# A Fourier mixing layer followed by a gated feed-forward: the first batch's rows on neighbouring partitions, and another order of the first steps

## The chip, the cores and the metric

The kernel runs on one core of a Trainium2 chip. A core has five engines that run their own instruction streams: TensorE (matmuls; PE in the profile, its weight loads PEld), VectorE (DVE), ScalarE (ACT), GpSimd (POOL) and SyncE (SP), which only issues transfers here. ScalarE issues some transfers too. Sixteen DMA engines move the data. On-chip memory has 128 partitions; the matmul results go to eight banks of 128 x 512 f32.

The metric is the device time of one launch in microseconds, the median of several runs. Each is one launch that does all of the work, weight preparation included.

## The reference

```python
def _attn_ref(x):                       # x: (8, 3008, 256), float32
    X = np.fft.fft(x, axis=1)
    X = np.fft.fft(X, axis=2)
    return X.real.astype(np.float32)

def _moe_ref(x, w_in, w_out):           # (24064, 256), (256, 2048), (2048, 256)
    h = x @ w_in
    g = h * (1.0 / (1.0 + np.exp(-1.702 * h)))
    return (g @ w_out).astype(np.float32)
```

The second takes the first's result as its 24064 rows. The kernel gets w_in and w_out in eight bytes for each number and makes floats of them itself.

## The kernel before

**Tiling.** The length 3008 is split as NA * NB = 47 * 64. A first stage transforms over the 47 (matmuls whose weights hold the cosines and sines), its result is spilled to a buffer Td in DRAM and read back in another layout (fill, into t4), and a second stage (stage2) transforms over the 64 and is turned by VectorE's transposes into pq. The transform over the 256 columns is never done on the data: it is multiplied into w_in once (fold_w, four pieces of 512 columns, result in wcs). After that the kernel is a feed-forward: hidden (matmuls of pq with wcs), rows (VectorE builds the second half of the hidden rows by symmetry, with the row nb that nyquist makes, and writes them to a ring "h" of four buffers), activate (the gated activation on ScalarE), product (matmuls with wo).

**Loops.** There are 8 batches * 3 blocks * 2 halves * 8 pairs = 384 steps. The first NP = 8 steps use plain products; from step 8 on the products with w_out are done by a scheme with seven products instead of eight, applied twice (the lines L621 to L701 of the profile).

**Who orders the work.** All instructions are in the order in which the program text issues them on each engine; there is no scheduler. A list SCRIPT says what is issued between the steps 0 to 7. Semaphores follow from what writes and reads what. Transfers take turns on eight semaphores, so that a transfer also waits until the one eight issues before it has landed.

**Start of the program (L864 to L945).** The rows of batch 0 go straight from x to a tile xt: load_first puts 48 rows (one for each of the 47, and one more) on partitions 0, 2, ... 94, load_mirror puts the mirrored rows on 33, 35, ... 127. Seven memsets clear xt ahead of it, since the matmuls read all 128 partitions. tab1, the table with the weights of this first stage, is loaded on 128 partitions in two parts. SP issues load_first, ScalarE load_mirror. Then w_in(0) (in two halves), tab2 and w_in(1) follow on SP. fold_first (VectorE) folds the columns in groups of four, mix_first (TensorE) makes two slots at a time and ScalarE copies them to buffers made[k], of which three are the first three buffers of the ring "h". After every second one, spill_first sends 16 of the 48 rows of both halves to Td, one half on SP's queue and one on ScalarE's. When all is there, fill(0, 0, 4) reads the first third of t4 back. The other 32 rows are spilled later on SP, behind w_out(0) and w_in(2).

**Weights.** A piece of w_in or w_out is made a float in five operations: sizes (absolute value of the high words, on ScalarE or VectorE), clamp (GpSimd), low (the low words, ScalarE), high (two operations on VectorE), finish (GpSimd, into wst for w_in and wo for w_out). halved(n) makes sum and difference of the two halves of a piece on VectorE, so that fold_w(n) needs four matmuls of 512 columns rather than eight. fold_w(0) is without it. first_row(n) makes small factors af1 and af2 out of wcs.

**Around the change.** Before step 0 come, in this order: in1's preparation, fold_w(0), halved(1), rotate (psr, the first matmul that needs t4), out0's preparation, stage2(0, 0), first_row(0), high(out0), load_in(3), finish_out(0), fold_w(1). In the steps: in2 in steps 0 and 1, product(0) and (1), out1 and in3 in step 3.

**Banks.** A matmul result takes a bank by the name of a tag: o0, o1 are kept for the products of a block's end, the six others are taken in turn from a list `spare`; a call may also name its bank.

```python
    def bank(name, tag=None):
        if tag is None:
            tag = spare.pop(0)
            spare.append(tag)
```

A warm matmul (L348) is one whose result is not used.

Of the kernel before, what the change touches and what calls it, by code (L numbers as in the profile page):

```python
# [34 lines left out]
NA, NB = 47, 64  # L35
# [26 lines left out]
def tables(S, D):  # L62
# [14 lines left out]
    low, high, back = w0[0:2 * NA:2], np.zeros((NA, NJ + 1, NG * NU, 2)), NJ - np.arange(1, NJ)  # L77
# [3 lines left out]
    w0[33:33 + 2 * NA:2] = high  # L81
    sign = np.ones((128, 4))
    sign[33:33 + 2 * NA:2] = -1.0
# [36 lines left out]
def kernel(ctx: ExitStack, tc, x, w_in, w_out, tab1, tab2, out):  # L120
# [162 lines left out]
    def at_rows(first, at, *dims):  # L283
        one = xt[first:first + 1]
        return bass.AP(one.tensor, one.offset + at * D, [[2 * xt[:].ap[0][0], NM]] + [list(d) for d in dims])
# [6 lines left out]
    def load_mirror(k):  # L292

        parts = ((1, 4), (28, 32)) if k == 0 else ((4 * k, 4 * k + 4), (28 - 4 * k, 32 - 4 * k))
        for lo, hi in parts:
            nc.scalar.dma_start(out=at_rows(33, lo, [D, hi - lo], [1, D]),
                                in_=view(x, (NB - lo) * D, [NB * D, NM], [-D, hi - lo], [1, D]))
        if k == 0:
            nc.sync.dma_start(out=at_rows(33, 0, [1, D]), in_=view(x, NJ * D, [NB * D, NM], [1, D]))
# [6 lines left out]
    def fold_first(g):  # L306

        t, e = xt[:, 4 * g:4 * g + 4, :], room[g]
        fwd, rev = t[:, :, 1:H], free(t, D - 1, [D, 4], [-1, H - 1])
        nc.vector.tensor_tensor(e[:, :, 0:H - 1], fwd, rev, op=ALU.subtract)  # L310
        if g not in BY_PE:
            nc.vector.tensor_tensor(fwd, fwd, rev, op=ALU.add)

    def mix_first(i):

        ps, ns = bank("ps1"), (2 * i + 2, 2 * i + 1) if i < 7 else (0, 15)
        for at, n in enumerate(ns):
            todo = [], []
            for c, slot in enumerate((n, NJ - n if n else 16)):
                o = ps[64 * c:64 * c + 64, at * D:(at + 1) * D]  # L320
                even, odd_ = (w[:, k * NM:k * NM + 64] for w, k in ((w0, slot), (odd, slot or NJ)))
                todo[c].append((o[:, H + 1:], odd_, room[slot // 4][:, slot % 4, 0:H - 1], True, True))
                folded = slot // 4 not in BY_PE
                todo[c].append((o[:, 0:H + 1], even, xt[:, slot, 0:H + 1], True, folded))
                if not folded:
                    todo[c].append((o[:, 1:H], even, free(xt[:, slot], D - 1, [-1, H - 1]), False, True))
# [40 lines left out]
    def stage2(b, blk):  # L367
# [14 lines left out]
        for u in range(NU):  # L382
            for cs in range(parts):
# [111 lines left out]
    def fold_w(n):  # L495
# [10 lines left out]
        for cs in range(2):  # L506

            nc.scalar.copy(wcs[cs][:, n * 512:(n + 1) * 512].rearrange("p (f c) -> p f c", f=4),
                           free(ps[cs][:], 0, [1, 4], [4, 128]))
# [344 lines left out]
    odd, w0 = flat[:, 0:n0], flat[:, 6176:6176 + n0 + 4]  # L854
# [10 lines left out]
    for lo, hi in (28, 32), (24, 28), (20, 24), (8, 12), (12, 20):  # L865
        nc.gpsimd.memset(xt[:, lo:hi, :], 0.0)
    nc.vector.memset(xt[:, 0:4, :], 0.0)
    nc.vector.memset(wcs[0][:, 0:512], 1.0)
    nc.vector.memset(xt[:, 4:8, :], 0.0)
    nc.vector.memset(ones[:], 0.0)  # L870
    nc.vector.memset(ones[0:1, :], 1.0)
    nc.scalar.activation(af2[0:1, 0:1], twos[0:1, 0:1], ACTF.Gelu_apprx_sigmoid)
# [3 lines left out]
                      in_=view(tab1, 0, [tab1.shape[1], 128], [28 * NM, 2], [1, ends]))  # L876
    for i in range(4):
        load_first(i)
        load_mirror(i)
        if i == 0:  # L880
            nc.sync.dma_start(out=w0[:, ends:28 * NM], in_=tab1[:, ends:28 * NM])
        if i == 1:
            odd_weights(NM, ends)
            odd_weights(28 * NM, n0)
# [9 lines left out]
    for i, need in enumerate(((0, 7), (1,), (6,), (2,), (5,), (3,), (4,), ())):  # L894
# [6 lines left out]
        if i % 2:  # L901
            spill_first(i // 2, 0, 16, (nc.sync, nc.scalar))
# [18 lines left out]
    sizes(in1, nc.vector)  # L921
    low(in1)
    for h0 in (0, 512):
        clamp(in1, h0, 512)
    for h0 in (0, 512):
        high(in1, h0, 512)
    for h0 in (0, 512):
# [3 lines left out]
    warm(1)  # L931
    fold_w(0)
    halved(1)
    rotate(0, 0, 4, nc.scalar.copy)
    prepare(out0)
    sizes(out0, nc.scalar)
    clamp(out0)
    low(out0)
    stage2(0, 0)
    first_row(0)  # L940
    spare.append(spare.pop(0))
    high(out0)
    load_in(3, nc.sync)
    finish_out(0)
    fold_w(1)  # L945
# [11 lines left out]
    for t, c in ((1, 2), (3, 3)):  # L957
        at(t, load_out, c, nc.sync)
# [13 lines left out]
    for b in range(B):  # L972
# [26 lines left out]
        for blk in range(NBLK):  # L999
# [7 lines left out]
        [(prepare, in2), (low, in2), (nyquist, 0, 0), (rows, 0, ((sizes, in2, nc.vector), (clamp, in2)))],  # L1007
        [(first_row, 1), (activate, 0), (rows, 1), (high, in2), (finish, in2)],
        [(activate, 1), (rows, 2), (halved, 2)],
        [(product, 0, 0, None), (product, 1, 0, None), (bounds, out1), (activate, 2), (bounds, in3), (rows, 3), (activate, 3),  # L1010
         (fold_w, 2), (high, out1), (finish, out1), (high, in3), (finish, in3)],
# [4 lines left out]
    for t in range(n + LAG):  # L1016
        if t < NP:
            if t == NP - 3:
                spare[:] = [tag for tag in spare if tag[0] == "o"] + ["b2"]
# [96 lines left out]
```

## Time and profile before

| | us |
|---|---|
| median of 3 runs | 1845.98 (1845.35 to 1847.09) |
| the profiled execution, whole | 1845.24 |
| its span, first to last instruction | 1843.5 |
| TensorE's mean granted clock | 0.997 of full |

The start of the profiled execution, by its trace:

| what | us from the span's start |
|---|---|
| clearing of xt on GpSimd | 0.73 to 6.1 |
| first loads of x issued (SP, ScalarE) | 2.05, 1.99 |
| last load of load_first landed | 16.4 |
| last mirrored rows landed | 19.39 |
| w_in(0), its halves landed | 20.42, 21.86 |
| last spill of 16 rows issued, landed (ScalarE) | 24.21, 26.58 |
| the same on SP | 24.20, 27.4 |
| fill of t4 issued, landed | 27.50, 31.59 |
| w_out(0), w_in(2) landed | 34.08, 38.70 |
| hidden(0), first matmul | 38.15 |
| product(0), first matmul | 47.26 |
| fold_w(1), fold_w(2), fold_w(3) on TensorE | 34.84, 54.16, 65.49 |

How to read the profile: the page has one execution, engine by engine, and the line of the program for each group of instructions (L191 is the helper `halves`, which records many matmuls; the tile's name tells which). The chain of waits follows the end of the execution back, at each step to what released it. A group's "waited for" tells which engine, line and tile ended an idle stretch. In the windows, each engine's busy time is followed by the number of its instructions; PEclk is the share of full speed that TensorE's clock had, and the DMA share is the mean busy share of the sixteen DMA engines.

### The profile page before, as it was taken

The numbers are of one execution on the slowest core, as the hardware profiler recorded it, in microseconds if no ns is written. First come the engines' busy times: TensorE is split into PE (matmuls) and PEld (weight loads), VectorE is DVE, ScalarE is ACT, GpSimd is POOL, SyncE is SP. The second block draws the span as 40 slices with busy tenths as digits, with TensorE's granted clock in tenths as the row PEclk, the third lists the DMA queues.
The fourth block names the chain that finished last, engine by engine and source line by source line (L and its number), as shares of the span: only waits on it lengthen the run. The fifth ranks groups of instructions, "written<-read, shape, count | busy, mean of one in ns | idle before, by whom it ended". The sixth has DMA issues, their size and how long they took to land.

```text
span 1843.5 us, 55849 instructions
## 1 busy us (share of the span) xinstructions
PE 1826.2 (99%) x23650; PEld 1398.9 (76%) x23650; DVE 1479.1 (80%) x1930; ACT 1139.4 (62%) x2231; POOL 997.7 (54%) x1068
## 2 busy tenths in 40 slices
PE   8999999999999999999999999999999999999998
PEld 4677777777777777777777777777777877778776
DVE  6888788887888778877888778878888788878874
ACT  4666656666666666666666666666656666556663
POOL 3785555554656546564456644666446654444442
PEclk9999999999999999999999999999999999999999
DMA  8721331114211151211502115020241102100101
GB/s 276 189 70 26 90 65 28 55 32 106 43 48 40 35 112 30 61 35 45 111 13 73 33 50 97 23 72 26 75 74 28 29 26 59 28 19 13 23 19 24
DMA packets 150841, 105.95 MB, mean 57 GB/s; under 512 B 106197, under 2 KB 131799, under 8 KB 150032
## 3 DMA queue, kind: packets, MB, share of 16 engines
q1 hardware_dynamic: 147760, 100.33, 22.6%
q8 instruction: 186, 3.05, 0.7%
q10 hardware_dynamic: 2832, 2.05, 0.5%
q14 instruction: 63, 0.52, 0.1%
HBM read 65.07 MB, written 48.05 MB: 61 GB/s over the span
## 4 chain that ended last, share of the span: by engine, by line
PE 95%; POOL 2%; DMA 1%; DVE 1%; issue 0%; ACT 0%; ACTq 0%; DVEq 0%; POOLq 0%; SPq 0%
PE x L191 35%; PE o L191 26%; PE low L701 25%; PE o L701 4%; PE ps L268 2%; PE ps L378 1%; DMA xt<-in_x_dram 1%; PE po L191 0%; DMA big<-in_moe_w_in_dram 0%; PE psw L501 0%; POOL wo L475 0%; PE pa L191 0%; POOL wo L493 0%; POOL big L632 0%; DMA t<-Td 0%
## 5 line engine op out<-in xcount | busy, mean ns | idle before, releaser
L632 POOL TENSOR_TENSOR big<-big 128x256 f32<-128x256 f32 (+1 forms) x376 | 353.6, 940 | 785.7 <-ACT big L624 672.2
L191 PE MATMUL x<-pq,wcs 128*64 128x256 f32 (+1 forms) x6016 | 768.8, 376 | 1.5 <-ACT g L614 0.9
L191 PE MATMUL o<-big,wo 128*64 128x256 f32 (+1 forms) x4800 | 621.0, 375 | 0.5 <-DVE big L639 0.5
L191 PEld LDWEIGHTS x<-pq,wcs 128*64 128x64 f32 x6016 | 414.1, 137 | 181.4 <-issue 15.6
L614 ACT ACTIVATE g<-x 128x512 f32<-128x512 f32 (+1 forms) x376 | 221.7, 590 | 380.1 <-PE x L191 378.9
L191 PEld LDWEIGHTS o<-big,wo 128*64 128x64 f32 x4800 | 341.8, 137 | 146.8 <-DVE big L639 0.9
L633 POOL TENSOR_TENSOR big<-big 128x256 f32<-128x256 f32 (+1 forms) x376 | 411.2, 1094 | 0.0
L621 DVE TENSOR_TENSOR big<-g,x 128x512 f32<-128x512 f32 (+1 forms) x376 | 250.7, 667 | 183.6 <-ACT big L617 183.4
L602 ACT ACTIVATE x<-nb,af 128x256 f32<-128x256 f32 (+1 forms) x752 | 353.0, 469 | 70.1 <-DVE pq L385 57.0
L701 PE MATMUL low<-big 128*64 128x128 f32 (+1 forms) x5888 | 381.4, 270 | 0.0
L701 PEld LDWEIGHTS low<-big 128*64 128x64 f32 x5888 | 336.9, 137 | 28.2
L617 ACT ACTIVATE big<-x 128x512 f32<-128x512 f32 (+1 forms) x376 | 219.2, 583 | 122.2 <-PE x L191 112.2
L663 DVE TENSOR_TENSOR big<-big 128x1024 f32<-128x1024 f32 (+1 forms) x184 | 235.4, 1280 | 65.9 <-PE low L701 43.1
L624 ACT ACTIVATE big<-big 128x512 f32<-128x512 f32 (+1 forms) x376 | 231.6, 616 | 34.9 <-DVE big L621 32.6
L701 PE MATMUL low<-big,wo 128*64 128x128 f32 (+1 forms) x2944 | 220.3, 270 | 0.1
L665 DVE TENSOR_TENSOR big<-big 128x512 f32<-128x512 f32 (+1 forms) x184 | 179.6, 976 | 16.3 <-DVE big L663 0.5
L667 DVE TENSOR_TENSOR big<-big 128x512 f32<-128x512 f32 (+1 forms) x184 | 184.0, 1000 | 0.0
L701 PEld LDWEIGHTS low<-big,wo 128*64 128x64 f32 x2944 | 171.8, 137 | 4.2 <-DVE big L667 0.5
L640 DVE TENSOR_TENSOR big<-big 128x512 f32<-128x512 f32 (+1 forms) x188 | 143.3, 762 | 6.5
L639 DVE TENSOR_TENSOR big<-big 128x512 f32<-128x512 f32 (+1 forms) x188 | 131.2, 698 | 3.5 <-POOL big L632 3.5
L803 DVE TENSOR_TENSOR big<-big,low 128x512 f32<-128x512 f32 (+3 forms) x184 | 109.0, 609 | 3.8
L701 PEld LDWEIGHTS o<-big,wo 128*64 128x64 f32 x1472 | 92.3, 137 | 24.9
(104 smaller groups left out, 1100.5 us busy)
## 6 DMA issues: line engine op xcount, KB each, us to landing
out_dram<-os SPq DMA_DIRECT2D x284, 64.0 KB
t<-Td SPq DMA_DIRECT2D x22, 512.0 KB
Td<-xt SPq DMA_DIRECT2D x56, 192.0 KB
xt<-in_x_dram SPq DMA_DIRECT2D x14, 512.0 KB
xt<-Xr SPq DMA_DIRECT2D x14, 512.0 KB
nb<-Nd SPq DMA_DIRECT2D x23, 256.0 KB
out_dram<-os SPq DMA_DIRECT2D x96, 56.0 KB
Xr<-in_x_dram SPq DMA_DIRECT2D x7, 752.0 KB
```

The costliest lines, as they stand in the source:

```text
L191: nc.tensor.matmul(out[c0:c0 + 64], lhsT=lhs[:, c0:c0 + 64], rhs=rhs, skip_group_check=True, **how)
L602: nc.scalar.activation(x[:, i * 256:i * 256 + n], nbt[b, blk][:, hh * 256:hh * 256 + n], ACTF.Copy, scale=af1[:, f:f + 1])
L614: nc.scalar.activation(two(g[:], n), two(xb[t][:], n), ACTF.Copy, scale=2.0)
L617: nc.scalar.activation(front(t), two(xb[t][:], width(t)), ACTF.Gelu_apprx_sigmoid)
L621: nc.vector.tensor_tensor(back(t), two(gt.pop(t)[:], n), two(xb.pop(t)[:], n), op=ALU.subtract)
L624: nc.scalar.activation(back(t), back(t), ACTF.Gelu_apprx_sigmoid)
L632: eng.tensor_tensor(right(t, S1, n), left(t, A21, n), right(t, A22, n), op=ALU.add)
L633: eng.tensor_tensor(left(t, S3, n), left(t, A11, n), left(t, A21, n), op=ALU.subtract)
L663: nc.vector.tensor_tensor(free(big[:], SUM, *both_), free(big[:], from11 + w, *twice), free(big[:], from11, [at_right(t, 0) + w - from11, ...
L665: nc.vector.tensor_tensor(s2, a11, s1, op=ALU.subtract)
L667: nc.vector.tensor_tensor(s4, a12, s2, op=ALU.subtract)
L701: nc.tensor.matmul(o, lhsT=lhs, rhs=rhs, start=first_in, stop=(p == NP - 2), skip_group_check=True)
```

## The change

1. The rows of batch 0 lie on partitions 0 to 47 and their mirrored rows on 48 to 95, and all operations of the first stage read 96 partitions. The seven memsets of xt are gone; tab1's first part is loaded on 96 partitions.
2. The load of ScalarE's activation table (with a first Gelu of one element) stands behind its first four transfers instead of ahead of them.
3. Both halves of the first spills are issued on ScalarE's queue.
4. The sizes of in1 are made on ScalarE in two halves of 512, not on VectorE in one; its low comes later. fold_w(0) is issued without its copies; the two copies (keep) stand before and behind rotate.
5. Ahead of step 0 only stage2(0, 0) and first_row(0) are left. out0's preparation, halved(1) and load_in(3) are in step 0, fold_w(1) and in2's sizes in step 1, in2's high and finish in step 3, with load_out(2) and load_out(3), which were tied to steps 1 and 3.
6. After fold_w(0) the list of spare banks is written out by name, 22 entries long; at step 5 it is set to four names.
7. In stage2's first block the four transposes go by column half first.

```diff
-    w0[33:33 + 2 * NA:2] = high
+    w0[NM:NM + NA] = high
...
     def at_rows(first, at, *dims):
         one = xt[first:first + 1]
-        return bass.AP(one.tensor, one.offset + at * D, [[2 * xt[:].ap[0][0], NM]] + [list(d) for d in dims])
+        return bass.AP(one.tensor, one.offset + at * D, [[xt[:].ap[0][0], NM]] + [list(d) for d in dims])
...
-        for u in range(NU):
-            for cs in range(parts):
+        for cs in range(parts):
+            for u in range(NU):
...
-    def fold_w(n):
+    def fold_w(n, copy=True):
...
-        for cs in range(2):
-
-            nc.scalar.copy(wcs[cs][:, n * 512:(n + 1) * 512].rearrange("p (f c) -> p f c", f=4),
-                           free(ps[cs][:], 0, [1, 4], [4, 128]))
+        folded_w[n] = ps
+        if copy:
+            keep(n, 0)
+            keep(n, 1)
+
+    folded_w = {}
+
+    def keep(n, cs):
+        nc.scalar.copy(wcs[cs][:, n * 512:(n + 1) * 512].rearrange("p (f c) -> p f c", f=4),
+                       free(folded_w[n][cs][:], 0, [1, 4], [4, 128]))
...
-    for lo, hi in (28, 32), (24, 28), (20, 24), (8, 12), (12, 20):
-        nc.gpsimd.memset(xt[:, lo:hi, :], 0.0)
-    nc.vector.memset(xt[:, 0:4, :], 0.0)
     nc.vector.memset(wcs[0][:, 0:512], 1.0)
-    nc.vector.memset(xt[:, 4:8, :], 0.0)
...
-    nc.scalar.activation(af2[0:1, 0:1], twos[0:1, 0:1], ACTF.Gelu_apprx_sigmoid)
...
-                      in_=view(tab1, 0, [tab1.shape[1], 128], [28 * NM, 2], [1, ends]))
+                      in_=view(tab1, 0, [tab1.shape[1], 2 * NM], [28 * NM, 2], [1, ends]))
...
         if i == 1:
+            nc.scalar.activation(af2[0:1, 0:1], wcs[0][0:1, 0:1], ACTF.Gelu_apprx_sigmoid)
...
-            spill_first(i // 2, 0, 16, (nc.sync, nc.scalar))
+            spill_first(i // 2, 0, 16, (nc.scalar, nc.scalar))
...
     prepare(in1)
-    sizes(in1, nc.vector)
-    low(in1)
     for h0 in (0, 512):
+        sizes(in1, nc.scalar, h0, 512)
         clamp(in1, h0, 512)
     for h0 in (0, 512):
         high(in1, h0, 512)
+    warm(1)
+    fold_w(0, False)
+    spare[:] = ["b0", "b1", "b2", "o2", "b0", "o3", "o4", "o2", "b1", "b2", "o4", "b0", "o3", "b2", "o4", "o2", "b0", "b1", "o3", "b2",
+                "o2", "o4"]
+    keep(0, 0)
+    rotate(0, 0, 4, nc.scalar.copy)
+    keep(0, 1)
+    low(in1)
     for h0 in (0, 512):
         finish_in(1, h0, 512)
     load_out(1, nc.sync)
     fill(0, 4, NG)
-    warm(1)
-    fold_w(0)
-    halved(1)
-    rotate(0, 0, 4, nc.scalar.copy)
-    prepare(out0)
-    sizes(out0, nc.scalar)
-    clamp(out0)
-    low(out0)
     stage2(0, 0)
     first_row(0)
-    spare.append(spare.pop(0))
-    high(out0)
-    load_in(3, nc.sync)
-    finish_out(0)
-    fold_w(1)
...
-    for t, c in ((1, 2), (3, 3)):
-        at(t, load_out, c, nc.sync)
...
     SCRIPT = (
-        [(prepare, in2), (low, in2), (nyquist, 0, 0), (rows, 0, ((sizes, in2, nc.vector), (clamp, in2)))],
-        [(first_row, 1), (activate, 0), (rows, 1), (high, in2), (finish, in2)],
-        [(activate, 1), (rows, 2), (halved, 2)],
-        [(product, 0, 0, None), (product, 1, 0, None), (bounds, out1), (activate, 2), (bounds, in3), (rows, 3), (activate, 3),
-         (fold_w, 2), (high, out1), (finish, out1), (high, in3), (finish, in3)],
+        [(prepare, out0), (sizes, out0, nc.scalar), (clamp, out0), (nyquist, 0, 0), (low, out0), (halved, 1), (rows, 0), (high, out0),
+         (load_in, 3, nc.sync), (finish, out0)],
+        [(fold_w, 1), (first_row, 1), (activate, 0), (rows, 1), (prepare, in2), (sizes, in2, nc.vector), (clamp, in2)],
+        [(activate, 1), (rows, 2)],
+        [(low, in2), (high, in2), (load_out, 2, nc.sync), (finish, in2), (activate, 2), (bounds, out1), (prepare, in3),
+         (sizes, in3, nc.scalar), (clamp, in3), (rows, 3), (activate, 3), (low, in3), (halved, 2), (product, 0, 0, None),
+         (product, 1, 0, None), (fold_w, 2), (high, out1), (load_out, 3, nc.sync), (finish, out1), (high, in3), (finish, in3)],
...
             if t == NP - 3:
-                spare[:] = [tag for tag in spare if tag[0] == "o"] + ["b2"]
+                spare[:] = ["o4", "o2", "o3", "b2"]
```

More of the change, by code (lines that the diff above doesn't have):

```diff
@@ L76, in tables @@
     w0 = np.zeros((128, NJ + 1, NG * NU, 2))
-    low, high, back = w0[0:2 * NA:2], np.zeros((NA, NJ + 1, NG * NU, 2)), NJ - np.arange(1, NJ)
+    low, high, back = w0[0:NA], np.zeros((NA, NJ + 1, NG * NU, 2)), NJ - np.arange(1, NJ)
     low[:] = w1[:, :NJ + 1]
@@ L80, in tables @@
     high[:, e0, :, 1], high[:, o0, :, 1] = cos[:, NJ], -sin[:, NJ]
-    w0[33:33 + 2 * NA:2] = high
+    w0[NM:NM + NA] = high
     sign = np.ones((128, 4))
-    sign[33:33 + 2 * NA:2] = -1.0
+    sign[NM:] = -1.0
     c, q = np.divmod(np.arange(NJ), 16)
@@ L295, in load_mirror @@
         for lo, hi in parts:
-            nc.scalar.dma_start(out=at_rows(33, lo, [D, hi - lo], [1, D]),
+            nc.scalar.dma_start(out=at_rows(NM, lo, [D, hi - lo], [1, D]),
                                 in_=view(x, (NB - lo) * D, [NB * D, NM], [-D, hi - lo], [1, D]))
         if k == 0:
-            nc.sync.dma_start(out=at_rows(33, 0, [1, D]), in_=view(x, NJ * D, [NB * D, NM], [1, D]))
+            nc.sync.dma_start(out=at_rows(NM, 0, [1, D]), in_=view(x, NJ * D, [NB * D, NM], [1, D]))
     def odd_weights(lo, hi):
@@ L306, in fold_first @@
     def fold_first(g):
-        t, e = xt[:, 4 * g:4 * g + 4, :], room[g]
+        t, e = xt[0:2 * NM, 4 * g:4 * g + 4, :], room[g][0:2 * NM]
         fwd, rev = t[:, :, 1:H], free(t, D - 1, [D, 4], [-1, H - 1])
@@ L321, in mix_first @@
                 even, odd_ = (w[:, k * NM:k * NM + 64] for w, k in ((w0, slot), (odd, slot or NJ)))
-                todo[c].append((o[:, H + 1:], odd_, room[slot // 4][:, slot % 4, 0:H - 1], True, True))
+                todo[c].append((o[:, H + 1:], odd_, room[slot // 4][0:2 * NM, slot % 4, 0:H - 1], True, True))
                 folded = slot // 4 not in BY_PE
-                todo[c].append((o[:, 0:H + 1], even, xt[:, slot, 0:H + 1], True, folded))
+                todo[c].append((o[:, 0:H + 1], even, xt[0:2 * NM, slot, 0:H + 1], True, folded))
                 if not folded:
-                    todo[c].append((o[:, 1:H], even, free(xt[:, slot], D - 1, [-1, H - 1]), False, True))
+                    todo[c].append((o[:, 1:H], even, free(xt[0:2 * NM, slot], D - 1, [-1, H - 1]), False, True))
             for k in range(3):
@@ L853 @@
     flat = wot[:].rearrange("p w a q n -> p (w a q n)")
-    odd, w0 = flat[:, 0:n0], flat[:, 6176:6176 + n0 + 4]
+    odd, w0 = flat[0:2 * NM, 0:n0], flat[0:2 * NM, 6176:6176 + n0 + 4]
     first = tp.tile([128, NG, D], F32, tag="t4", name="first")
@@ L880 @@
         if i == 0:
-            nc.sync.dma_start(out=w0[:, ends:28 * NM], in_=tab1[:, ends:28 * NM])
+            nc.sync.dma_start(out=w0[:, ends:28 * NM], in_=tab1[0:2 * NM, ends:28 * NM])
         if i == 1:
+            nc.scalar.activation(af2[0:1, 0:1], wcs[0][0:1, 0:1], ACTF.Gelu_apprx_sigmoid)
             odd_weights(NM, ends)
```

## The prediction

> **What bounds the kernel now.** I read the page first, for the share of each engine.
>
> ```profile
> PE 1826.2 (99%) x23650; PEld 1398.9 (76%) x23650; DVE 1479.1 (80%) x1930; ACT 1139.4 (62%) x2231; POOL 997.7 (54%) x1068
> ```
>
> TensorE is busy for 1826.2 of 1843.5 us, so the loop is bound by its matmuls, and the change touches none of the loop after step 7. It can only move the point at which TensorE comes to the steady loop. I therefore read the start of the chain of waits next.
>
> ```profile
> 0.73 3.50 POOL xt L866 x4
> 4.23 10.67 DMA xt<-in_x_dram
> 14.92 5.50 DMA big<-in_moe_w_in_dram
> ...
> 24.20 3.17 DMA Td<-e
> 27.50 4.08 DMA t<-Td
> ...
> 34.84 3.52 PE psw L501 x8
> ...
> 47.26 6.91 PE o L191 x64
> ...
> 59.97 2.37 POOL wst L467
> ```
>
> Columns: start, length, what. GpSimd's clearing of xt, the loads of x, the spill of e and the fill of t follow one another until 31.6 us. Then TensorE leads to about 59, and from there GpSimd and VectorE, which build the weights, lead until about 115. So an idle stretch of TensorE before 115 us is worth something only if the weights come earlier too. The waits of TensorE in the first 120 us:
>
> ```profile
> PE psr L191 <- DMA t<-Td: 2.6, 1, 2.6
> PE pb L191 <- DVE big L589: 1.9, 1, 1.9
> ```
>
> The first is the fill; the second is hidden(5), at 59.23 to 61.04 us, waiting for a bank that rows(4) still reads. Then the windows (PE, PEld, DVE, ACT, POOL busy, clock, DMA share, GB/s):
>
> ```profile
> 4.00:19.00 15.00, 14.40 (x89) 7.59 (x88) 7.25 (x11) 3.89 (x7) 2.09 (x2) 1.00 1.04 272
> 20.00:25.00 5.00, 4.22 (x61) 3.22 (x57) 4.28 (x7) 3.69 (x7) 2.52 (x3) 1.00 1.02 400
> 31.80:38.70 6.90, 6.90 (x96) 3.84 (x98) 4.70 (x9) 3.36 (x7) 2.48 (x3) 0.51 0.95 368
> 72.00:73.00 1.00, 1.00 (x12) 0.71 (x10) 0.00 (x0) 1.00 (x3) 1.00 (x2) 1.00 1.06 209
> 75.00:77.00 2.00, 2.00 (x22) 1.43 (x20) 2.00 (x4) 1.12 (x3) 0.69 (x1) 1.00 1.05 104
> ```
>
> The DMA engines are full from 4 to 19 us at 272 GB/s; w_in(1), on 128 partitions, gets 400; the later loads of x into 32 partitions get 209, those into 15 get 104, all at a full share. The clock is half from 31.87 to 38.70 us, right after the 2.53 us in which TensorE waited for the fill.
>
> **The change part by part.**
>
> *Clearing and the smaller table.* The seven memsets of xt go. Their cover was nothing: the first load of x is issued at 2.05 us on SP and 1.99 on ScalarE, behind the memsets. Without them SP is free at 0.74 + 0.46 = 1.2 and ScalarE at about 0.74. That is 0.85 to 1.25 us, and since the DMA engines are full afterwards, what starts earlier stays earlier. The table's first part goes from 802 KB to 602 KB: 200 KB at 272 GB/s is 0.74 us. Together -1.6 to -2.0; I take -1.8. The activation-table load moves from the head of ScalarE behind four issues; it costs nothing there, because the first fold starts at 8.05 us and ScalarE waits for it.
>
> *Neighbouring partitions.* Before, 48 rows lie on every second partition of 0 to 94 and 48 on 33 to 127, so that each half of the memory gets as many. After, the rows take 0 to 47 and 48 to 95, so 64 rows lie in the lower 64 partitions and 32 above. No row shows a load into 48 or 96 neighbours. Upper bound of the cost: both queues together are held to the 209 GB/s of 32 partitions. x (3.08 MB) and the table (0.60 MB) take 3.68 MB / 209 = 17.6 us in place of 13.5 at 272: +4.1. Lower bound: only the lower half is held to 209, 64 rows of 32 KB and 6.3 KB of table, 2.46 MB, 11.8 us; the rest runs beside it and the 13.5 us stand: 0. Between the two I take the middle, +2.1, since the rows of 32 and of 15 partitions show a rate that falls with the number of partitions, and 48 is much nearer to 32 than to 128. Sum of the two edits: +0.3, ends -2.0 and +2.5.
>
> The Trainium skill (SBUF — State Buffer, section "Door 1: The DMA port swizzle (why [64,N] ≈ [32,N])") says that partitions 0 to 63 reach one set of eight of the sixteen ports and 64 to 127 the other, so that 64 neighbours load no faster than 32. The rows of 209, 104 and 400 GB/s agree with it. By its map, as an estimate, the busiest ports get 313 KB after the change and 248 KB before, which at 209 / 8 = 26 GB/s is 12.0 and 9.5 us: +2.5 in place of +2.1.
>
> *w_in earlier.* The transfers take turns on eight semaphores, and by the new order the first half of w_in(0) waits for another one (landed at 10.9 us; before, 14.90). It can be issued some 3 us earlier, but it stands on SP's queue behind the last x load (landed 16.4), so it gains nothing, and it may run beside the last mirrored rows. 0, ends -0.5 and +0.5.
>
> *Spills.* Both halves go out on ScalarE's queue. There the last spill took 26.58 - 24.21 = 2.37 us, on SP, behind w_in(1), 3.17 (the chain above). The second is issued 0.36 us after the first: 24.57 + 2.4 = 27.0 in place of 27.4. So the fill starts 0.3 us earlier, and w_out(0), w_in(2) and the 32-row spills behind it on SP too. ScalarE's four further issues of 0.36 fall into its gaps (busy 3.69 of the 5 us from 20 to 25); without that cover, one of them delays the last copies by 0.36. Value -0.3, ends -0.5 and +0.1.
>
> *Steps 0 and 1 ahead of fold_w(1).* TensorE's work is the same. What matters is VectorE, which before runs:
>
> ```profile
> 36.40 0.69 DVE L454 TENSOR_SCALAR big<-big 128x1024 uint32<-128x1024 uint32 x1 [0.45 <-POOL big L435]
> 37.13 1.23 DVE L455 SCALAR_TENSOR_TENSOR big<-big 128x1024 uint32<-128x1024 uint32 x1
> 40.42 0.69 DVE L582 TENSOR_TENSOR big<-v,pb 128x512 f32<-128x512 f32 x1 [2.06 <-PE pb L191]
> 45.45 0.68 DVE L454 TENSOR_SCALAR big<-big 128x1024 uint32<-128x1024 uint32 x1
> 50.00 1.52 DVE L480 TENSOR_TENSOR big<-wst 128x512 f32<-128x512 f32 x1 [0.49 <-POOL wst L467]
> ```
>
> The first pair is high(out0), then rows(0) after 2.06 us of idle time in which TensorE did fold_w(1) and hidden(0), then high(in2) and halved(2). After, hidden(0) needs only the four transposes, which could end at about 34, so rows(0) could start before 38. But rows(0) writes the first of the four h buffers, and the 32-row spill of the first pair reads it. That spill lies on SP's queue behind w_out(0) and w_in(2); by the records of its packets its two halves land at 39.1 and 39.4 us. So a transfer takes the place of the wait: rows(0) starts at 39.1 (with the 0.3 of above), -1.3. Then I walk VectorE with its own durations: 2.1 for a rows, 1.9 for a high, 0.7 for sizes. Rows(0) to 41.2; high(out0), which was ahead, to 43.1; rows(1) to 45.2 (before 45.45); sizes(in2) to 45.9; rows(2) to 48.0; high(in2) to 49.8 (before 47.3). GpSimd's finish of in2 takes 2.4, to 52.2; rows(3) runs beside it, then halved(2) to 53.6, or 54.4 if GpSimd runs beside it (1.52 in place of 0.69 above), and high(out1) to 55.5 or 56.3, where before it ended at 56.0. So the point from which GpSimd and VectorE lead comes 0.5 earlier to 0.3 later. The move of in1's sizes to ScalarE (0.68 twice, while ScalarE waits) costs nothing, the later fill of product(0) neither, since rows(3) is later anyway. But GpSimd is left idle from about 37.5 to 43, and finish(out0) ends at 45.6 instead of 41.05; product(0) began at 47.26, so 1.6 us of cover are left. Were these gone, each us that finish(out0) is late would be a us of TensorE. With the half clock, which the fill's wait leaves in force, hidden(0) and the nyquist matmuls may end at about 40 and not before 39: 0 to +0.8. Value +0.5 with the 0.3 of the spills in it, ends -0.5 and +1.1.
>
> *Named banks.* The 1.81 us before hidden(5)'s pb can go, since rows(4) no longer holds its bank. What is late next is hidden(6), which takes a bank of fold_w(3): that needs wst (GpSimd 59.97 to 62.34), halved(3) to 63.66, 1.72 of matmuls and ScalarE's copies (66.77 to 68.0). None of it comes earlier. TensorE would run up to it sooner and wait there. Value 0, ends -1.8 and 0. The transposes' new order changes nothing: hidden(0)'s pb needs all four.
>
> Sum: +0.3 + 0 + 0.5 + 0 = about +0.8. Against the profiled execution (span 1843.5 and 1.74 around it, 1845.24) that makes 1846.0; it lies 0.74 below the median of the runs, 1845.98, so the median would be 1846.8.
>
> **The rivals.**
>
> *A second stretch at half clock (slower).* If the named banks let TensorE run up to hidden(6), the 1.81 us of idle time and the 0.3 that the trace has there become one wait of about 2.1 to 2.4 at 65 to 68 us. For it: 2.53 us of waiting at 29.09 was followed by 6.83 us at half the clock. Against it: 1.81 us at 59.23 was not. It decides from somewhere between 1.81 and 2.53 us within one stretch of 3.41 (6.83 is two of them). 6.83 us at half cost 3.4; 1846.8 + 3.4 = 1850.2.
>
> The Trainium skill (TensorE: Matmul & The Clock Gate) describes such windows of about 3.4 us that run on their own; the 6.83 us agrees, and so this is a matter of where the wait falls in a window.
>
> *The partitions cost the upper bound (slower by less).* Both queues at 209 GB/s: +4.1 in place of +2.1. Against it: the 400 GB/s of whole loads shows that the upper half has its own share. 1846.8 + 2.0 = 1848.8.
>
> *Faster.* The partitions cost nothing (x is 1.8 earlier), the walk takes its early end (-0.5), and half of the bank's 1.81 is kept. For it: at 272 GB/s the first loads were already well below the 400 of a whole load, so what holds them may be something that the partitions don't touch. -1.8 - 0.5 - 0.9 = -3.2: 1842.8.
>
> *It does not do what it says:* the loads still wait (for a semaphore of an earlier one), so clearing gains nothing, and x is late by the partitions' +2.1. It falls together with the second rival.
>
> **How the numbers follow.** Forecast 0.50, second half clock 0.19, partitions 0.14, faster 0.17. A difference under 0.2% (3.7 us) is what a measurement of this kernel can't tell from none. The forecast's own range is 1844.5 to 1848.7. The time is 1846.8; the range 1842.6 to 1850.4 takes in the rivals' times and leaves less than 2 in 10 outside. Faster by over 0.2% (under 1842.3) needs the faster case and more: 0.15. Slower by over 0.2% (above 1849.7) needs the second half clock, or the partitions with the cold start: 0.28. Same 0.57.
>
> **What would show it.** In the profile after: the first loads of x issued before 1.3 us; the last mirrored rows landing within 2 us of 19.39; the DMA rate from 4 to 19 us between 209 and 272; the wait of psr for the fill still over 2 us; VectorE's L588 (rows(0)) starting at 39 and high(out0) behind it; no wait of hidden(5)'s pb, but one of 2 us or more at hidden(6); the clock full at 60 to 80 us. The forecast is wrong if rows(0) starts before 37.5 (then the spill did not hold it), if x lands 3 us earlier or later, or if the clock falls to half a second time.

## The result

| | median of the runs, us | against the kernel before on the same chip |
|---|---|---|
| before | 1846.37 (1844.75 to 1848.18, 8 runs) | |
| changed | 1852.27 (1849.63 to 1853.22, 8 runs) | +5.90, ratio 1.003, 95% interval 1.002 to 1.0041 |

The change makes the kernel 5.9 us slower. The profiled execution took 1852.13 us with a span of 1850.3, 6.8 more than the span before. The first line of the page, busy time by engine:

```profile
PE 1829.5 (99%) x23650; PEld 1398.0 (76%) x23650; DVE 1477.7 (80%) x1927; ACT 1140.3 (62%) x2233; POOL 991.7 (54%) x1063
```

TensorE is busy for 3.3 us more with the same matmuls, and the other 3.5 us of the span are waiting. All of it comes at the start: the matmul that stands at 57 us before is 7.9 us later, and the last one 6.9. The chain of waits of the changed kernel, 0 to 130 us (start, length, what):

```profile
2.18 8.43 DMA xt<-in_x_dram
10.62 14.70 DMA xt<-in_x_dram
...
31.06 2.02 DMA Td<-e
33.34 4.03 DMA t<-Td
...
45.89 1.74 PE psw L501 x8
...
60.37 1.52 DVE big L481
```

There is no clearing at its head now, but the last mirrored rows, issued at 10.62 us, need 14.70 us to land, at 25.32 in place of 19.39. The spill of e is a shorter step, as was forecast (2.02 in place of 3.17), but the run with the old spills below has 2.14, so this is not the work of the queue. The fill is issued at 33.34 in place of 27.50: 5.84 us later, nearly the whole loss. The windows of the changed kernel (busy PE, PEld, DVE, ACT, POOL, clock, DMA share, GB/s):

```profile
4.00:19.00 15.00, 12.56 (x79) 6.73 (x79) 5.89 (x9) 3.84 (x8) 0.00 (x0) 1.00 1.05 194
...
59.00:80.00 21.00, 17.69 (x162) 10.15 (x160) 16.93 (x22) 12.79 (x21) 14.30 (x11) 1.00 0.74 228
```

The DMA engines are full, as before, but move 194 GB/s where they moved 272. From 59 to 80 us the clock is full, but earlier it is at half twice:

```profile
25.90:32.70 6.80, 6.59 (x34) 3.94 (x36) 4.86 (x7) 4.32 (x9) 3.22 (x4) 0.50 0.50 151
...
39.50:43.00 3.50, 3.20 (x16) 1.87 (x18) 1.77 (x5) 1.44 (x5) 2.49 (x2) 0.51 1.02 358
```

The records have these two stretches from 25.92 to 32.75 and from 39.58 to 42.99 us, 10.24 us together in the first 130 us, against 6.83 before. At half speed the 3.41 us more are 1.7 us of matmul work, about half of the 3.3. What TensorE waited for in the first 120 us:

```profile
PE ps L330 <- DVE first L310: 3.4, 3, 1.7
PE pa L191 <- ACT wcs L514: 1.7, 1, 1.7
PE ps L330 <- DVE big L310: 1.6, 2, 1.3
PE psr L191 <- DMA t<-Td: 1.5, 1, 1.5
...
PE psw L501 <- DVE big L480: 1.3, 1, 1.3
```

The first stage (ps L330) now waits for its rows. The wait of hidden(5) is gone; one of 1.7 us has come before hidden(6) (pa, for ScalarE's copies of fold_w(3)), and one of 1.3 before fold_w(2) (psw, for halved(2)).

### The profile page after: what moved, and what is told of

It is laid out like the page before. It is cut to its first block, busy times and chain, and to the rows that moved or that the text cites. A ratio compares the mean times of both kernels' runs of the same rounds, so it can differ in the third digit from the quotient of the medians.

```text
span 1850.3 us, 55827 instructions
## 1 busy us (share of the span) xinstructions
PE 1829.5 (99%) x23650; PEld 1398.0 (76%) x23650; DVE 1477.7 (80%) x1927; ACT 1140.3 (62%) x2233; POOL 991.7 (54%) x1063
## 4 chain that ended last, share of the span: by engine, by line
PE 94%; POOL 2%; DMA 2%; DVE 1%; issue 1%; ACT 0%; ACTq 0%; DVEq 0%; SPq 0%; POOLq 0%
PE x L191 34%; PE o L191 26%; PE low L707 25%; PE o L707 4%; PE ps L268 2%; PE ps L378 1%; DMA xt<-in_x_dram 1%; POOL wo L475 0%; PE po L191 0%; DVE big L455 0%; POOL wo L493 0%; POOL wst L467 0%; POOL big L638 0%; DMA t<-Td 0%; PE ps L330 0%
```

## The experiments

Each kernel was timed in five rounds against the kernel before on the same chip; the difference given is that of the two medians. An interval reaches about 1.7 us to either side, and the runs lie on four chips, so by an estimate from these widths two runs must differ by some 2.4 us before the difference between them is clear of the spread. Landing times and clocks are those of the one profiled execution, where nothing else is said. The parts are called rows (item 1 of the change), table load (2), spills (3), order (4, 5, 7) and banks (6).

### Old rows in the changed kernel

```diff
-        return bass.AP(one.tensor, one.offset + at * D, [[xt[:].ap[0][0], NM]] + [list(d) for d in dims])
+        return bass.AP(one.tensor, one.offset + at * D, [[2 * xt[:].ap[0][0], NM]] + [list(d) for d in dims])
...
+    for lo, hi in (28, 32), (24, 28), (20, 24), (8, 12), (12, 20):
+        nc.gpsimd.memset(xt[:, lo:hi, :], 0.0)
```

> The changed kernel with batch 0's rows back on every second partition, the clearing and the 128-partition table of before; spills, order and banks stay as changed. Partitions theory (the slow landing of x is the whole loss): the last mirrored rows land at 18.5 to 20 us in place of 25.3, the fill is issued at about 27.2 in place of 33.35, and the time is within 1.5 us of before (ratio 0.999 to 1.001). Order theory (the order of steps 0 to 3 and the banks cost as well): x lands as before but the time stays 2 us or more above it (ratio over 1.001).

1847.34 us, +0.72 against before (ratio 1.0004, 0.9995 to 1.0013). The mirrored rows landed at 19.45, the fill was issued at 27.98. So the rows, beside the rest of the change, carry 5 of the 5.9 us, and the partitions theory's number holds. The time stays a little above before, within the interval, though the spills should have gained; what the order costs is asked below.

### New rows alone

```diff
 # the kernel before, with
+        return bass.AP(one.tensor, one.offset + at * D, [[xt[:].ap[0][0], NM]] + [list(d) for d in dims])
...
-    for lo, hi in (28, 32), (24, 28), (20, 24), (8, 12), (12, 20):
-        nc.gpsimd.memset(xt[:, lo:hi, :], 0.0)
```

> The kernel before with the rows on 96 neighbouring partitions, no clearing and the table on 96, and nothing else of the change. By the order of issue the first half of w_in(0) waits for the fourth mirrored load here, as before, and not for the table's second part as in the changed kernel. Partitions theory: the mirrored rows land at 24 us or later all the same, and the time is 4.5 to 7 us above before (ratio 1.0025 to 1.0038). Theory of w_in(0) (its earlier issue, at 10.1 us, is what keeps the mirrored rows back): they land by 22 and the time is at most 3 us above.

1847.47 us, +0.85 (ratio 1.0005, 0.9996 to 1.0014). This is what the theory of w_in(0) allows (at most 3 us), and far from the partitions theory; the landing, at 22.35, is 0.35 later than it said. The fill was issued at 30.53, 3.0 us later than before, and yet the time rose by 0.85 only. The rate from 4 to 19 us, in this kernel:

```profile
4.00:19.00 15.00, 13.13 (x79) 7.32 (x79) 6.57 (x10) 3.68 (x7) 0.00 (x0) 0.89 1.09 201
```

So the new rows are slow by themselves (201 GB/s against 272), but 3 us of the delay in the changed kernel come only together with something else. Two questions: what adds 3 us, and whether something hid 2 us here.

### w_in behind the rows

```diff
-    load_in(0, nc.sync, ((0, 1), (1, 2)))
-    nc.sync.dma_start(out=small[:, :CD + 4 * H], in_=tab2[:])
-    load_in(1, nc.sync)
+    load_in(0, nc.scalar, ((0, 1), (1, 2)))
+    nc.scalar.dma_start(out=small[:, :CD + 4 * H], in_=tab2[:])
+    load_in(1, nc.scalar)
...
-            spill_first(i // 2, 0, 16, (nc.scalar, nc.scalar))
+            spill_first(i // 2, 0, 16, (nc.sync, nc.sync))
```

> The changed kernel with w_in(0), tab2 and w_in(1) issued on ScalarE's queue behind the mirrored rows, and the first spills on SP. Nothing can then stand before the last rows but the rows themselves. Theory of w_in(0): the mirrored rows land at about 20 us, 5 us earlier than in the changed kernel, and the time falls by 3 to 5 us. Partitions theory: 64 of 96 rows in the lower half at about 209 GB/s take 11.8 us from about 3 us on, so the rows could land at 16 to 20 too, but w_in(0) comes later by as much and the time falls by 2 us at most.

1851.06 us, +4.44 (ratio 1.0023, 1.0014 to 1.0033). The mirrored rows landed at 21.34, four us earlier than in the changed kernel, but w_in(0)'s second half landed at 25.71 and not 23.27, w_in(1) at 29.95, and the last spill, whose turn waited for w_in(1), at 31.83: the fill came only 1.3 us earlier, and the time fell by 1.5, not by the 3 to 5 of the theory. It left the question open, since it moved all of w_in.

### Old spills in the changed kernel

```diff
-            spill_first(i // 2, 0, 16, (nc.scalar, nc.scalar))
+            spill_first(i // 2, 0, 16, (nc.sync, nc.scalar))
```

> The changed kernel with the first spills on SP and ScalarE, one half each, as before. By the prediction's term the last spill lands 0.3 us later and the time is 0.3 us above the changed kernel. If the pair on one queue has become the slower one (in the changed kernel packets of the spills took 340 to 390 ns in place of 159), the time falls by up to 0.5 us. Both are near the spread of the runs.

1852.47 us, +5.85 (ratio 1.0031, 1.0019 to 1.0042): as the changed kernel. Here the spills are worth nothing that can be seen.

### The table load, from both sides

Transfers take turns on eight semaphores. The built program of the changed kernel has the first mirrored load ahead of the table, since ScalarE no longer loads its activation table first. With that, the turn of w_in(0)'s first half is that of the table's second part (landed at 10.11 us), where before it was that of the fourth mirrored load (14.90). Once added to the new rows alone, once taken back in the changed kernel:

```diff
 # new rows alone, with
-    nc.scalar.activation(af2[0:1, 0:1], twos[0:1, 0:1], ACTF.Gelu_apprx_sigmoid)
...
         if i == 1:
+            nc.scalar.activation(af2[0:1, 0:1], wcs[0][0:1, 0:1], ACTF.Gelu_apprx_sigmoid)
```

> The kernel before with the new rows (as the earlier run of them alone) and, in addition, the activation table's load moved behind ScalarE's first four transfers. With that move the first mirrored load comes first in the order in which transfers take turns on the eight semaphores, and the first half of w_in(0) waits for the table's second part (landed at about 10) rather than for the fourth mirrored load (about 14). Theory of the turns: w_in(0) is issued at about 10, the last mirrored rows land at about 25 in place of 22.35, the fill is issued at about 33 in place of 30.5, and the time is 2 to 3.5 us above that run (about 1850). Rival (the spills' queue or ScalarE's issues make the rest of the delay): rows, fill and time stay as in that run.

1850.41 us, +3.46 (ratio 1.002, 1.0011 to 1.0029): 2.6 above the new rows alone. w_in(0) was issued at 10.53, the mirrored rows landed at 26.67, the fill was issued at 34.32.

```diff
 # the changed kernel, with
+    nc.scalar.activation(af2[0:1, 0:1], twos[0:1, 0:1], ACTF.Gelu_apprx_sigmoid)
...
         if i == 1:
-            nc.scalar.activation(af2[0:1, 0:1], wcs[0][0:1, 0:1], ACTF.Gelu_apprx_sigmoid)
```

> The changed kernel with the activation table's load back at the head of ScalarE, and nothing else. Theory of the turns: w_in(0) is issued at about 14 again, the mirrored rows land at about 22.4, the fill is issued at 30 to 31 in place of 33.35, and the time is 2 to 3.5 us less than the changed kernel's (about 1849.5). Rival: nothing moves, the time stays at about 1852.

1849.51 us, +2.56 (ratio 1.0015, 1.0007 to 1.0024): 3.3 under the changed kernel. w_in(0) was issued at 13.25, the mirrored rows landed at 22.71, the fill was issued at 30.72. Rows and fill are both 2.6 us earlier than in the changed kernel. Both runs came out as the theory of the turns had them.

### One more transfer

This leaves the table load where the change puts it and adds one transfer of 1 KB ahead of w_in(0), so that w_in(0), and every transfer behind it, takes the next turn.

```diff
+    nc.sync.dma_start(out=Nd[0:1, 0:256], in_=view(x, 0, [D, 1], [1, D]))
     load_in(0, nc.sync, ((0, 1), (1, 2)))
```

> The changed kernel with one more transfer of 1 KB (a row of x into a buffer in DRAM that is written again later) issued on SP just ahead of w_in(0). It takes the turn that waits for the table's second part; w_in(0)'s first half then waits for the second load_first, which landed at 14.8. Theory of w_in(0)'s issue: it is issued at about 14.8 in place of 10.1, the mirrored rows land at 22 to 23 in place of 25.3, and the time falls by 2 to 3 us (about 1849.5), though a transfer is added and the activation table's load is where the change put it. Rival (the place of the table's load itself, or ScalarE's work, is what costs): the time stays at 1852 or rises.

1848.94 us, +2.29 (ratio 1.0012, 1.0003 to 1.0021): 3.6 under the changed kernel, with a transfer more. SP's issues, in order of time, first the changed kernel's, then this one's:

```profile
10.13 4.63 SPq L411 DMA_DIRECT2D big<-in_moe_w_in_dram  x2
```

```profile
10.10 0.63 SPq L889 DMA_DIRECT2D Nd<-in_x_dram  x1
14.69 0.36 SPq L411 DMA_DIRECT2D big<-in_moe_w_in_dram  x1
```

w_in(0) goes out at 14.69 in place of 10.13 (its second half at 17.4 in place of 14.41), and the mirrored rows land at 21.49 in place of 25.32. The packets show why. At 18 us the changed kernel has 430 of the 1 KB packets of the mirrored rows to go and this one 397. Here w_in(0)'s first packet after that comes at 19.55, and the 1 KB packets run at 203 and 182 in a microsecond and end at 20.56. In the changed kernel w_in(0) has sent from 17.83 on; they run at 43 to 83 until 22 us and end at 24.48. So w_in(0) beside the mirrored rows is what keeps them back by 3.8 us.

The profiled execution does not show the way from there to the 3.6 us of the medians:

```profile
17.46 11.48 PE ps L330 x106
...
32.23 4.04 DMA t<-Td
```

It is the slowest of the eleven (1850.69), TensorE ran at half clock from 17.66 to 27.90, and the fill came only 1.1 us earlier than in the changed kernel. Its clock over the whole execution is 0.996, where seven of the others have 0.999; the changed kernel's eight have 0.993 to 0.998. How much of the 3.6 came by way of the clock, which itself may hang on the waits for the rows, is not shown. In the run with the table load at the head, whose profiled execution is its median, fill and time go together: 2.6 us earlier and 3.3 us less, with 6.83 us at half clock against 10.24.

### Two unused matmuls in the wait for the fill

```diff
     fold_w(0)
+    warm(2)
+    spare.insert(0, spare.pop())
     halved(1)
```

First in the kernel before:

> The kernel before with two more matmuls of 0.86 us, whose result is not used, between fold_w(0) and the wait for the fill, in the bank that the next matmul takes anyway. Clock theory: the wait that is left is under 1 us in its stretch, the clock stays full from 31.87 to 38.70, and since 6.83 us at half cost 3.4 us of matmuls the time falls by 1.5 to 3.3 us. Rival (from 38 us on VectorE, GpSimd and the 32-row spills lead, not TensorE): it falls by less than 1 us, or not at all.

1845.64 us, -1.31 (ratio 0.9996, 0.9987 to 1.0005): just under the range of the clock theory, and its interval takes in no change. Its windows (the clock is the number before the last two):

```profile
31.80:38.70 6.90, 5.35 (x100) 3.30 (x100) 4.89 (x9) 2.15 (x3) 3.32 (x3) 1.00 0.96 370
...
59.00:66.00 7.00, 5.08 (x42) 3.20 (x42) 5.60 (x10) 4.03 (x7) 5.77 (x3) 0.76 1.00 305
```

The stretch at half clock from 31.87 to 38.70 is gone, but one of 3.41 us has come at 62, behind the wait of 1.81 us before hidden(5), which was not followed by one before. Then with the new rows:

> The kernel before with the new rows and, in addition, the two unused matmuls in front of the wait for the fill. The rows alone delayed the fill by 3.0 us and the time by 0.8 only. Masking theory (the late fill came with a full clock after it, where the kernel before ran 6.83 us at half): with the clock full in both, the rows cost their whole delay, and the time is 2 to 3.2 us above the run of the kernel before with the two matmuls (1845.6), so 1847.6 to 1848.8. Rival (something behind the fill swallows 2 us of any delay): it stays at 1846.4 or so, 0.8 above.

1847.67 us, +1.19 (ratio 1.0006, 0.9998 to 1.0015): 2.5 above the run just told, each set against its own runs of before. So by this pair the rows cost 2.5 us, not 0.85. A reason could be the clock: in the profiled execution of the new rows alone, the late fill came with a full clock (1.00 from 31.8 to 38.7 in its windows, 0.51 before). But that execution is the fastest of its eleven, and over all of them the mean clock is 0.997, under the 0.998 of before; so that the clock paid for the other 1.7 is not shown. The pair is not at one clock either (0.999 and 0.998 in the mean). Among the runs with 0.999 alone, seven and three, each against its own before, the rows cost 2.4.

### Clearing kept

```diff
 # new rows alone, with
+    for lo, hi in (28, 32), (24, 28), (20, 24), (8, 12), (12, 20):
+        nc.gpsimd.memset(xt[:, lo:hi, :], 0.0)
+    nc.vector.memset(xt[:, 0:4, :], 0.0)
...
+    nc.vector.memset(xt[:, 4:8, :], 0.0)
```

> The kernel before with the new rows and the 96-partition table, but with the seven memsets kept. By the prediction's term the clearing held x back by 0.85 to 1.25 us, and since the DMA engines are full afterwards the last rows land that much later than without it (23.2 to 23.6 in place of 22.35) and the time rises by about 1 from 1847.5. If the rate of the lower half's partitions is the limit from the first load on, the delay is the same. Rival (the first microseconds are limited by something else): the rows land at 22.4 and the time stays.

1848.67 us, +2.19 (ratio 1.0013, 1.0004 to 1.0022): 1.3 above the new rows alone, within the spread. That is the size forecast, but not its mechanism: in the profiled execution the rows landed at 22.01 and the fill was issued at 30.43, no later than without the clearing. The clock was at half for 3.41 us from 18.6, from 28.9 and from 63.0. Whether the 1.3 is the clearing or the clock is not settled.

### The order and the banks

The kernel before with spills and table load alone differs from the changed kernel with the old rows by order and banks:

```diff
 # the kernel before, with
-            spill_first(i // 2, 0, 16, (nc.sync, nc.scalar))
+            spill_first(i // 2, 0, 16, (nc.scalar, nc.scalar))
...
-    nc.scalar.activation(af2[0:1, 0:1], twos[0:1, 0:1], ACTF.Gelu_apprx_sigmoid)
...
+            nc.scalar.activation(af2[0:1, 0:1], wcs[0][0:1, 0:1], ACTF.Gelu_apprx_sigmoid)
```

> The kernel before with the first spills on ScalarE's queue and the activation table's load moved, nothing else (old rows, old order, banks in turn). It differs from the changed kernel with the old rows (1847.3) by the order of the first steps and the banks alone. By the prediction's terms: the fill 0.3 earlier than before, the time 0.3 below before, and the order adds 0.2 to 0.8. Order theory: this run is 0 to 0.5 below before and the order costs 1 us or more; rival: this run is itself 0.5 or more above before, and the order costs nothing.

1845.10 us, -1.38 (ratio 0.9993, 0.9984 to 1.0001). Against the +0.72 with order and banks, these two cost 2.1 us, a little less than what is clear of the spread. With the spills alone:

> The kernel before with the first spills on ScalarE's queue and nothing else. The prediction's term: the last spill lands 0.3 to 0.4 us earlier and the time falls by 0.3 (1846.2). If the whole 1.4 us of the run with both edits are the spills', it is at about 1845.1, and in its profile the fill is issued more than 0.4 us before 27.5 or the clock is halved for a shorter time. If they are the table load's, the time stays at 1846.5.

1846.30 us, -0.35 (ratio 0.9997, 0.9988 to 1.0006): the size that was forecast, but well within the spread, and not by the mechanism. The fill was to be issued 0.3 us earlier than at 27.50; in the profiled execution (1846.74) it came 1.74 us later:

```profile
29.24 0.38 SPq L358 DMA_DIRECT2D t<-Td  x1
```

The other 1.0 of the run before stands beside the table load and is within the spread too; there the fill was issued at 27.50, as before. With the table load, by the turns, the second half of w_in(0) was issued at 15.2 and not at 18.2 as in the run with the spills alone; beside the old rows no harm of this can be seen.

What in the order costs, read from VectorE's timeline of the changed kernel (start, length, engine, line, operation):

```profile
45.08 0.69 DVE L588 TENSOR_TENSOR big<-v,pb 128x512 f32<-128x512 f32 x1 [1.65 <-PE pa L191]
...
58.94 1.52 DVE L480 TENSOR_TENSOR big<-wst 128x512 f32<-128x512 f32 x1 [0.49 <-POOL wst L467]
60.37 1.52 DVE L481 TENSOR_TENSOR big<-wst 128x512 f32<-128x512 f32 x1
```

and from GpSimd's:

```profile
56.52 2.39 POOL L467 TENSOR_TENSOR wst<-big 128x1024 uint32<-128x1024 uint32 x1 [3.00 <-DVE big L455]
58.87 2.48 POOL L435 TENSOR_SCALAR big<-big 128x1024 f32<-128x1024 f32 x2
```

halved(2) (L480, L481) runs beside two clamps now and takes 1.52 twice, where 0.69 and 0.68 are its times alone. So one of the clamps was moved into the 3.00 us in which GpSimd was idle:

```diff
-        [(low, in2), (high, in2), (load_out, 2, nc.sync), (finish, in2), (activate, 2), (bounds, out1), (prepare, in3),
+        [(low, in2), (prepare, out1), (sizes, out1, nc.scalar), (clamp, out1), (high, in2), (load_out, 2, nc.sync), (finish, in2), (activate, 2),
+         (low, out1), (prepare, in3),
```

> The changed kernel with the old rows, and out1's sizes and clamp moved ahead of high(in2) and finish(in2), where GpSimd was idle for 3 us. Theory of the port between VectorE and GpSimd (halved(2) took 1.52 twice instead of 0.69 and 0.68, beside the two clamps): one of the two falls to 0.7, TensorE's wait before fold_w(2) (1.13) shrinks by 0.8, and the time falls by 0.5 to 1.0 from 1847.3. Rival (this wait is made good later, GpSimd's chain leads): no change within 0.3.

1846.55 us, +0.07 (ratio 1.0001, 0.9992 to 1.001): 0.65 under the changed kernel with the old rows, inside the range of the theory but less than the spread. What the edit does to halved(2) is seen in its timeline of VectorE:

```profile
55.80 1.51 DVE L480 TENSOR_TENSOR big<-wst 128x512 f32<-128x512 f32 x1 [1.19 <-POOL wst L467]
57.24 0.68 DVE L481 TENSOR_TENSOR big<-wst 128x512 f32<-128x512 f32 x1
```

Last, the banks in turn (the list at step 5 is the old one again as well, and so is the turn of the list ahead of step 0):

```diff
 # the changed kernel with the old rows, without
-    spare[:] = ["b0", "b1", "b2", "o2", "b0", "o3", "o4", "o2", "b1", "b2", "o4", "b0", "o3", "b2", "o4", "o2", "b0", "b1", "o3", "b2",
-                "o2", "o4"]
```

> The changed kernel with the old rows (as the earlier run of it, 1847.3) and with banks taken in turn in place of the two written lists. Prediction's term (a named bank only moves the wait): a wait of 1.5 to 2 us before hidden(5) comes back, the one before hidden(6) (1.74) goes or shrinks by as much, and the time is within 0.7 us of that run. If the lists themselves cost or gain something, it differs by 1 us or more.

1848.29 us, +1.34 (ratio 1.001, 1.0001 to 1.0019): 0.6 above the same with the lists, but with a wide spread (1847.04 to 1852.06). TensorE's waits from 40 to 80 us, in this kernel:

```profile
PE pb L191 <- DVE big L595: 2.4, 2, 1.7
PE psw L501 <- DVE big L595: 1.5, 1, 1.5
```

and in the changed kernel with the old rows, which has the lists:

```profile
PE pa L191 <- ACT wcs L514: 1.7, 1, 1.7
PE psw L501 <- DVE big L480: 1.2, 1, 1.2
```

The wait of hidden(5) is back and that of hidden(6) is gone: the lists move 1.7 us from one step to the next. That they gain something is not shown: behind both waits, at 75.2 us, the two profiled executions do the same matmuls 0.08 us apart, though the one with the lists had 3.41 us at half clock before and the other none.

### Spills, table load and the two matmuls together

The kernel before with spills, table load and the two unused matmuls:

> The kernel before with the first spills on ScalarE's queue, the activation table's load moved (1845.1 in the earlier run) and the two unused matmuls in front of the wait for the fill (1845.6 alone, 1.3 under before). If the two gains are of different kinds (a fill that starts earlier, a clock that stays full) they add: 1843.8 or so, 2.3 to 3 us under before. If both came from the clock (the earlier fill shortened the wait that halves it), the second adds nothing: 1845.

1844.98 us, -1.67 (ratio 0.999, 0.9981 to 0.9999). Its interval ends just under 1, but the two gains don't add: without the two matmuls it was -1.38, which the spread does not tell from this. Its clock was full at the fill and at half for 3.41 us from 60.9, behind the wait before hidden(5).

## Why the prediction was wrong

**The step that failed** is "w_in earlier", which stood at 0, with ends of -0.5 and +0.5. It had seen that w_in(0) would be issued some 3 us earlier (it was 4.8) and that it may run beside the last mirrored rows, and still took it for free, because w_in(0) stands behind the last x load on SP's queue. But the mirrored rows are on the other queue, and they were not done: they go in packets of 1 KB, w_in(0) in packets of 4 KB. Taking the early issue away with one small transfer gave 3.6 us back; taking the table load back gave 3.3; adding it to the new rows alone cost 2.6. Without the early issue the change is left with +2.3, which lies inside the forecast's own range (-1.5 to +2.7 around the 1845.98 of before); so this one term carried the time out of it, though the others are not all right either. The table load itself was costed by its engine alone ("it costs nothing there"); what it moved was the turn of another queue's transfer.

**The rows** were mis-sized: +2.1 for the partitions and -1.8 for the clearing made +0.3. With the two unused matmuls in both kernels, rows without clearing cost 2.5, the forecast's upper end (+2.5); without them they measured +0.85, and which of the two is their price is not settled. The forecast had bounded the rate from below by the 209 GB/s of 32 partitions; in 4 to 19 us the new rows got 194 to 201, with two queues running. So the rate was below that bound. The 1.8 for the clearing and the smaller table was not shown: the first loads were issued at 1.18 and 0.73 us, but with the clearing kept the rows landed no later. If nothing was gained there, the partitions' price by that pair is 2.5, near the middle; if 1.8 was, it is 4.3, at the upper bound (+4.1). The runs don't settle which.

The Trainium skill (SBUF — State Buffer, section "Door 1: The DMA port swizzle (why [64,N] ≈ [32,N])") says that 64 neighbouring partitions load no faster than 32. The 194 to 201 GB/s into 96 partitions, 64 of them in the lower half, stand beside the 209 of 32 partitions and go with it. They are less than its map alone would give: by the estimate of the prediction the 3.68 MB take 12.0 us, some 306 GB/s. So that its +2.5 is the 2.5 measured is luck; the 2.5 measured also has the missing clearing and the smaller table in it.

**The spills** came out in size, -0.35 alone for a forecast of -0.3, but by luck: the interval takes in no change, and in the profiled execution the fill was later and not earlier.

**The order** was under-sized: +0.8 forecast (the +0.5 has the -0.3 of the spills in it), 2.1 measured for order and banks together, from runs on two chips and near the spread. Its first half was right. The spill of the first pair does hold rows(0): the two halves landed at 44.96 us at the latest and VectorE's L588 started at 45.08; with the old rows at 39.37 and 39.49, with the table load at the head 42.17 and 42.30. The walk was right up to rows(1) (ended at 51.24, which is 45.4 when the fill's 5.84 is taken off; forecast 45.2). It then lost 0.5 at sizes(in2), which took 1.22 and not 0.7, and most at halved(2): forecast to end at 53.6 or 54.4, it ended at 61.89, or 56.0 with the 5.84 taken off. Both its operations ran beside a clamp and took 1.52, and the walk had priced one of them so. Moving one clamp away gave 0.65 back, within the spread. The rest of the 2.1 was not taken apart.

**The named banks** did what was said: hidden(5)'s wait went, hidden(6) waited 1.74 us, and the net is not told from 0 (0.6, in a wide spread).

**The rivals.** The second stretch at half clock did not happen where the rival put it: the wait before hidden(6) was 1.74, and the clock was full from 59 to 80 us. But a second one did happen, earlier (25.92 to 32.75 and 39.58 to 42.99 us), which the prediction had named as a sign of being wrong. At 25.92 it came behind waits of 1.24 and 1.32 us, so the rival's bound between 1.81 and 2.53 us does not hold for a single wait. In the kernels with the unused matmuls a stretch came where the rival had it, after 1.81 and 1.93 us. The rival of the partitions was right in kind and too small (+2.0), since it too left out w_in(0). "Faster" fell. Of "it does not do what it says" the reason fell, since the loads were issued earlier, but what followed from it, that the clearing gains nothing, is what the landing with the clearing kept shows.

## What to carry to other kernels

When transfers take turns on a few semaphores, an edit that moves any transfer, even by moving an operation in front of it, changes what all later ones wait for: list the turns before and after, and cost every transfer that goes out earlier against those still under way on the other queue. Here the rows that crowd one half of the partitions lost a quarter of the load rate (201 against 272 GB/s), and the cleared gap was the cheaper. And where a delay seems to cost less than its length, look at the clock of all executions, and not of the profiled one alone, before naming what hid the rest.

## What the runs showed of the hardware

The two queues did not share the DMA engines by bytes. From 18 to 22 us of the changed kernel, while w_in(0) went to 128 partitions on SP's queue, the records have 36 to 67 of its 4 KB packets in each microsecond and 43 to 83 of the mirrored rows' 1 KB packets: about one for one, so about four times the bytes for w_in(0). From 11 to 14 us, with load_first's 4 KB packets into the crowded half, they have 32 to 37 of these, at about 440 to 480 ns each, and only 2 to 15 of the 1 KB packets. In the kernel before it was 46 to 52 and 27 to 58 from 11 to 13 us, at about 270 and 70 ns. The Trainium skill (DMA: Bandwidth & Descriptors, section "Queues, rings and completion order") says that each DMA engine takes turns between its queues by packets of several descriptors. By that, the queue with the small ones gets the small share, as from 18 to 22 us; the shares from 11 to 14 us it does not explain, and why they were so low was not tried.

A wait of 1.81 us was once followed by a stretch of 3.41 us at half clock and once not, and waits of 1.24 and 1.32 us were followed by one of 6.83, so the length of a single wait does not decide it. The Trainium skill (TensorE: Matmul & The Clock Gate, section "Part 1: The HAM clock gate") has windows of about 3.4 us that run on their own; the stretches of 3.41, 6.83 and 10.24 us (17.66 to 27.90 in the run with the extra transfer), one, two and three of them, agree, and where in a window a wait falls was not controlled in any run.
